# Delta-rule attention and a multiplicative FFN on one core: odd heads' keys, X and masked scores back on their own partitions, and another order of steps

## The chip, the cores and the metric

One core of one Trainium2 chip. A core has five engines that run side by side, each through its own instructions in order: TensorE (PE in the profile, its weight loads PEld), VectorE (DVE), ScalarE (ACT), GpSimd (POOL) and SyncE (SP), which here only issues DMA transfers. They share SBUF, 128 partitions wide; TensorE writes to PSUM, 128 partitions by 8 banks of 512 floats. The metric is the device time of one execution in microseconds (us), as the median of several runs. All data that is computed with is float32; the inputs arrive as float64 for the weights.

## What is computed

```python
# attention: B, H, S, D = 4, 8, 768, 48; moe_w1, moe_w2: 384x1024; w3: 1024x1024; w_out: 1024x384
k_n = k / (np.linalg.norm(k, axis=-1, keepdims=True) + 1e-06)
state = np.zeros((B, H, D, D))
for t in range(S):
    kt, vt, bt = k_n[:, :, t], v[:, :, t], beta[:, :, t, None]
    y[:, :, t] = np.einsum('bhd,bhde->bhe', q[:, :, t], state)
    v_old = np.einsum('bhde,bhd->bhe', state, kt)
    state = state + bt[:, :, :, None] * np.einsum('bhd,bhe->bhde', kt, vt - v_old)
x = y.transpose(0, 2, 1, 3).reshape(B * S, H * D)      # 3072 tokens x 384
a = x @ w1
b = x @ w2
h = a * b @ w3
out = h @ w_out
```

## The kernel before

**Tiling.** The 768 time steps are cut into 12 chunks of C = 64. A tile of a chunk has 128 partitions: batch b = NR\*z + r stands with its 64 time steps on half z of the partitions, and r (2), the head h (8) and its 48 features run along the free dimension. Tiles in feature layout (KQ, S, the FFN's xT) have an even head's 48 features from partition 0 and an odd head's from partition 64. Within a chunk the recurrence becomes products: scores K·Kᵀ and K·Qᵀ, a triangular inverse T, X = T·(V − K·S) scaled by w, the new state S + Kᵀ·X, and the outputs S·Q + (masked scores)·X.

**TensorE in corners.** These products are small (contraction 48 or 64, 48 or 64 weight columns, 48 to 128 moved columns). Each is a 64x64 tile of the array; which of the four corners it uses is given by the partitions of its operands (rows) and by the partitions that it writes (columns). A float32 product shows as two records in the profile.

**What is crossed.** In this kernel the odd heads' keys of chunk m (`ktok`, loaded by `load_crossed`, L192, four DMAs a chunk), their X and their masked scores stand on the other half of the partitions. So the product that makes X (`crossed`, called in `products`, L517) reads half z and writes half (z + h) % 2; `scores` (L360 and L366) makes an odd head's two parts by two products of 64 columns, since they go to different halves; and `outputs` (L618) can issue all products of masked scores and X in the first of its two parts, where row half and bank agree. Between the two parts PE is drained. The sums of squares and the weights w are needed in both places; `across` (L251) moves the odd heads' values to the other half by two products with an identity and two VectorE copies.

**The steps.** Every piece of work is a generator: a step runs it to its next yield. `ORDER`, a text of step names written out, sets the order of the instructions on every engine; nothing is reordered after. The names: Pn converts a piece of a weight matrix (DMA of the raw float64 words; three ScalarE operations, L671 to L673, one of which takes the sign; a shift by 3 on VectorE, L675; a sum and a product on GpSimd, L677 and L678); tn transposes a piece of w3 and fn folds w3·w_out into w34 (L713, L722); kn, qn, vn, pn are loads (pn: 16 DMAs of k and q in another layout, L226); Kn and Qn transposes on TensorE for chunks 0 and 1, dn on VectorE for the others (L320); gn squares of two chunks (L266, L268) and Nn norms; sn scores; un the DMAs that gather the 32x32 diagonal blocks of two chunks for the inverse; Vn the inverse itself, 31 steps of two VectorE operations (L434, L439) on 128 blocks at once; en the corner of the inverse (four DMAs back, L464, L473, L480, L487, L494); nn the scaling of v on GpSimd (L503); cn the chain of chunk n (three calls of `products` at L517, VectorE operations between at L550, L560, L581); yn its outputs (L618, L639, and the DMAs that complete xT); auj the FFN's two first products and their product elementwise for two chunks u and 128 columns j (L742, L751, L756); oub the last product and the store (L762, L768).

**V0 and V1.** While an inverse runs its matrix can lie in SBUF (`Vb`) or in a pair of PSUM banks, with two ScalarE copies in and two out (L428, L443). Here the inverses j < 2 lie in PSUM; the pair of banks is one of two that scores, chains and outputs take in turn.

```python
        def crossed(ps, r, h, z):
            g = NP * r + h // 2
            return ps[half((z + h) % 2), h % 2, D * g : D * g + D]
```

Of the kernel before, what the change touches and what calls it, by code (L numbers as in the profile page):

```python
# [9 lines left out]
U32 = mybir.dt.uint32  # L10
ALU = mybir.AluOpType
# [26 lines left out]
P6 k0 q0 K0 g0 k1 beta K0 K0 K0 P0 P6 K0 g0 P11 g0 Q0 g0 Q0 g0 g0 g0 P6 P6 g0 q1 Q0 Q0 Q0 P0  # L38
P0 P0 K1 K1 K1 K1 P7 K1 V0 P11 beta g0 g0 k2 beta P7 N0 P7 P7 s0 s0 s0 Q1 Q1 Q1 Q1 P11 P11
s0 s0 Q1 s1 s0 s0 s1 s1 s1 P2 P2 P10 P10 P13 u0 s1 s1 u1 t3 N0 P4 P1 P13 P2 P2 V0 t3 P10 P10  # L40
t2 P13 N0 V0 V0 P4 P4 P4 P1 P1 P3 P3 P13 s1 v0 V0 t5 V0 V0 V0 t2 t5 V0 V0 P1 P3 P3 V0 V0 f1
V0 P12 P12 P12 P12 V0 V0 n0 t4 P5 P5 P14 P14 P5 P5 t4 f2 V0 V0 V0 P14 V0 V0 k3 V0 V0 P22 f1
s0 P22 P22 V0 V0 P23 P23 P23 V0 P15 p2 P15 P15 f1 f2 f2 P14 V0 t6 t6 P22 t14 t14 P23 t15 P20
P20 t15 f7 V0 V0 P21 P21 V0 V0 V0 V0 V0 V0 V0 P15 g1 g1 n0 g1 V0 V0 t7 P21 P21 d2 d2 f3 P16
f7 P16 P16 P19 t7 f3 g1 g1 P20 P20 p2 f7 d2 d2 s2 t12 t12 f3 P19 t13 g1 g1 g1 g1 V0 e0 e0 e0
e0 P8 g1 t13 N1 P9 s2 s2 s2 P16 t8 P19 e0 e0 p3 f6 s2 P8 P8 c0 c0 f6 s2 y0 e1 e1 e1 P9 P9 V1
P17 P17 P17 p3 f6 t8 y0 P19 t11 t11 P8 t0 P18 P18 d3 d3 d3 d3 v1 s3 s3 s3 P17 s3 s3 P25 t0
P9 u2 u3 V1 t9 c0 s3 s1 f4 e1 c0 t9 N1 N1 P18 e1 n1 n1 c1 c1 P18 f4 V1 V1 V1 V1 P25 P25 P25
e1 c1 f4 P26 P26 P26 P26 c1 P24 P24 t10 t10 P31 t1 V1 V1 V1 t1 V1 V1 v2 n2 n2 f0 P24 P24 P27
y1 V1 V1 V1 f0 y1 f5 c1 P27 V1 V1 V1 V1 P31 P31 P31 V1 P30 k4 P30 P30 f5 V1 P27 y1 P27 a00  # L50
P32 f0 V1 V1 f5 k5 P30 P28 V1 V1 P32 P32 P32 V1 V1 V1 V1 V1 P29 a03 a00 a03 P28 P28 a02 a01
V1 V1 g2 V1 V1 P28 g2 g2 a02 V1 V1 P29 p4 d4 P29 P29 a01 a01 a01 c1 a00 a00 V1 a02 a02 c2 g2
g2 g2 d4 p4 d4 V1 g2 V1 e2 e2 a03 d4 g2 a05 e2 c2 P33 a03 e3 P35 p5 g2 g2 N2 P33 P33 s4 s4
s4 s4 s4 a07 a05 e2 P35 e2 e2 e3 P35 P33 P35 s4 a07 a06 c2 c2 e3 P34 v3 n3 P34 a04 n3 P34 y2
y2 c2 P34 a05 c2 c3 d5 p5 d5 d5 e3 e3 d5 a04 a06 a06 c3 k6 u4 s5 s5 s5 p6 a06 s5 s5 a05 s5
u5 V2 V2 a07 a07 e3 c3 c3 a04 a04 y3 y3 c3 N2 N2 o02 o02 o02 g3 o00 o00 k7 o01 o01 V2 V2 V2
g3 V2 V2 V2 V2 V2 V2 V2 V2 V2 V2 V2 V2 V2 V2 V2 V2 V2 V2 o00 v4 n4 n4 o03 o03 y3 a17 a13 a10
a13 V2 p6 V2 V2 V2 V2 V2 V2 V2 V2 a17 a12 a12 V2 V2 e4 a10 e4 c3 a17 a15 a15 e4 a17 a13 a13
e4 c4 d6 d6 g3 e4 e4 g3 g3 a16 a16 p7 c4 c4 a11 c4 c4 c4 a15 a15 v5 a11 a12 e5 c5 d6 d6 n5
g3 a12 y4 y4 n5 g3 g3 k8 g3 c5 e5 a14 g3 N3 V3 s6 s6 s6 s6 v6 d7 d7 p7 d7 d7 a16 a16 e5 a14  # L60
a14 e5 e5 g4 e5 N3 a14 s6 s6 s7 o03 s7 s7 s7 s7 u6 u7 V3 s7 N3 a10 a10 v7 c5 c5 a11 a11 y5
y5 y5 o01 c5 c5 V3 V3 V3 V3 o10 o10 V3 V3 V3 V3 V3 V3 p8 p8 o13 V3 V3 V3 V3 a27 o13 o13 V3
V3 V3 V3 o12 V3 V3 d8 o10 V3 a27 V3 V3 V3 o12 o12 k9 V3 V3 a24 a24 V3 V3 V3 V3 V3 V3 e6 g4
g4 g4 g4 g4 o11 o11 d8 a24 a24 d8 a27 a27 g4 g4 a23 a23 e6 a23 a23 p9 d8 g4 n6 g4 c6 e6 s8
n6 c6 v8 a26 a26 N4 s8 a26 a26 s8 s8 s8 s8 e6 e6 e6 V4 a25 a25 c6 a22 a22 n8 c6 c6 c6 y6 y6
n7 e7 e7 n7 a25 a25 e7 a20 a20 d9 d9 p9 d9 d9 s9 s9 s9 p10 s9 s9 a22 a22 N4 p10 e7 e7 u8 u9
s9 N4 c7 c7 a20 a20 a21 e7 c7 k11 c7 a21 a21 a21 V4 y7 y7 y7 o23 o23 V4 V4 V4 o23 o11 c7 V4
V4 V4 k10 g5 V4 V4 V4 V4 V4 V4 V4 V4 V4 V4 o22 o22 o22 d10 d10 a37 a35 a35 V4 v9 V4 V4 V4 V4
a37 a31 a31 V4 V4 V4 a34 a34 o20 V4 n8 d10 V4 V4 V4 V4 V4 V4 V4 e8 o20 g5 g5 a35 o21 o21 c7
c8 e9 g5 g5 g5 g5 g5 g5 n9 n9 e8 d10 e8 e8 c8 a35 g5 N5 s10 v10 s10 s10 s10 s10 u10 s10 V5  # L70
e9 a37 e8 e8 a36 c8 c8 a37 p11 a36 a36 a36 p11 o20 y8 y8 c8 c8 a34 a34 e9 e9 d11 d11 a30 d11
d11 s11 s11 s11 s11 s11 s11 e9 c9 u11 a30 a30 e9 c9 c9 a30 c9 V5 a31 a31 a32 a32 y9 y9 y9 V5
V5 V5 V5 V5 V5 a33 a33 a33 n10 a33 o21 V5 V5 V5 V5 V5 V5 a32 a32 a47 a47 a40 a40 a42 o32 a41
a42 V5 V5 n10 V5 V5 V5 o32 o33 o33 a47 o32 o33 V5 V5 V5 V5 V5 V5 V5 V5 v11 n11 V5 V5 a41 n11
V5 V5 V5 V5 V5 a47 o30 o30 o30 a42 a42 a46 a40 e10 e10 e10 a46 c9 N5 o31 e10 e10 c9 c10 a40
a44 e10 c10 c10 N5 o31 o31 a44 a44 a44 a46 e11 c10 c10 y10 a45 e11 e11 c10 a45 a45 a46 a45
a41 e11 a43 y10 a43 a43 a43 e11 e11 c11 a41 o41 o41 o41 c11 c11 o40 o40 o40 c11 y11 y11 y11
o42 o42 o43 o42 a53 a53 o43 a53 a53 a52 a52 a52 a52 a50 a50 a50 a50 a54 a54 a54 a54 a55 a55
a55 a55 a51 a56 a56 a56 a51 a51 a56 a51 a57 a57 a57 o43 a57 o50 o50 o51 o52 o50 o52 o52 o51
o51 o53 o53 o53  # L80
# [4 lines left out]
def kernel(  # L85
# [107 lines left out]
    def load_crossed(src, m, dma, tag, bufs):  # L193

        t = in_turn(work, [P, NR, H, D], tag, bufs, tag)
        for z in range(2):
            for e in range(2):
                dma(
                    out=t[half(z ^ e)].rearrange("t r (a e) d -> t e (r a) d", e=2)[:, e],
                    in_=src.rearrange("(z r) (a e) t d -> z e (r a) t d", z=2, e=2)[  # L200
                        z, e, :, C * m : C * m + C, :
                    ].rearrange("g t d -> t g d"),
                )
        return t

# [36 lines left out]
    def across(src, dst):  # L242

        n = src.shape[1]
        ps = bank([P, n, NR, NP])
        odd, even = (
            x.rearrange("p c r (a e) -> p e (c r) a", e=2) for x in (src, dst)
        )
        psv = ps[:].rearrange("p c r a -> p (c r) a")
        for z in range(2):  # L250
            pe.matmul(  # L251
                psv[half(1 - z)], lhsT=ident[half(z), half(z)], rhs=odd[half(z), 1],
                start=True, stop=True,
            )
        yield
        dve.tensor_copy(out=even[:, 0], in_=odd[:, 0])
        dve.tensor_copy(out=even[:, 1], in_=psv)
        yield

    def squares(j):  # L260
        sums[j] = ss = in_turn(small, [P, 2, 2, NR, H], "ss", 1, "ss")
        for cc in range(2):
            kt = ktoks[2 * j + cc]
            for r in range(NR):
                sq = in_turn(work, [P, H, D], "sq", 1, "sq")
                pool.tensor_tensor(out=sq[:], in0=kt[:, r], in1=kt[:, r], op=ALU.mult)  # L266
                yield
                dve.tensor_reduce(out=ss[:, 1, cc, r], in_=sq[:], axis=AX.X, op=ALU.add)  # L268
                yield
        yield from across(ss[:, 1], ss[:, 0])  # L270

    def norms(j):
        ss = sums.pop(j)[:, 0]
        seed = in_turn(small, [P, 2, NR, H], "seed", 1, "seed", U32)
        dve.tensor_scalar(
            out=seed[:], in0=ss.bitcast(U32), scalar1=-0.5, scalar2=1597463007.0,
# [3 lines left out]
        for _ in range(3):  # L280
            t = in_turn(small, [P, 2, NR, H], "nt", 2, "nt")
            dve.scalar_tensor_tensor(
                out=t[:], in0=ss, scalar=-0.5, in1=r, op0=ALU.mult, op1=ALU.mult
# [8 lines left out]
        dve.tensor_tensor(out=n[:], in0=r, in1=ss, op=ALU.mult)  # L292
        dve.tensor_scalar(out=n[:], in0=n[:], scalar1=1e-6, scalar2=None, op0=ALU.add)
        inv = in_turn(small, [P, 2, NR, H], "inv", 1, "inv")
        dve.reciprocal(out=inv[:], in_=n[:])

        w = ws[j] = in_turn(small, [P, 2, 2, NR, H], "wt", 3, "wt")
        dve.tensor_tensor(out=w[:, 0], in0=inv[:], in1=inv[:], op=ALU.mult)
        dve.tensor_tensor(
            out=w[:, 0], in0=w[:, 0], in1=beta_tok[:, 2 * j : 2 * j + 2], op=ALU.mult  # L300
        )
        ns[j] = n
        yield
        yield from across(w[:, 0], w[:, 1])

    def scale_of(x, m, crossed=0):
        j, cc = divmod(m, 2)
        return x[j][:, cc] if x is ns else x[j][:, crossed, cc]
# [17 lines left out]
    def by_tensor(m, i, src):  # L326
        KQ = KQs[m] if m in KQs else new_KQ(m)
        ps = [bank([P, NR, NP, C]) for z in range(2)]
        for r in range(NR):
            for h in range(H):  # L330
                for z in range(2):
                    x = half(z if i else (z + h) % 2)
                    pe.matmul(
                        ps[z][feat(h % 2), r, h // 2, :], lhsT=src[x, r, h, :],
                        rhs=ident[x, x], start=True, stop=True,
                    )
# [14 lines left out]
    def scores(m):  # L351
        for r in range(NR):
            KQ = KQs[m]
            ps = two_banks()
            for h in range(H):
                for z in range(2):
                    x = KQ[feat(h % 2), NR * z + r, h // 2]
                    n = 128 * (h // 2)
                    if h % 2 == 0:
                        pe.matmul(  # L360
                            ps[half(z), 0, n : n + 128], lhsT=x[:, 0, :],
                            rhs=x.rearrange("p j t -> p (j t)"), start=True, stop=True,
                        )
                    else:
                        for j in range(2):
# [520 lines left out]
```

## Time and profile before

| | |
|---|---|
| median of 3 runs (lowest, highest) | 611.42 us (610.54, 613.09) |
| the profiled execution | 610.54 us, span 608.8 us |
| mean granted TensorE clock | 0.969 |
| bytes moved by DMA | 55.67 MB, 91 GB/s in the mean |
| FFN's first products, L742 | 132.7 + 131.1 us busy on PE |
| FFN's last product, L762 | 127.3 us busy on PE |

The span is the time from the first to the last instruction in one profiled execution. A busy time counts an engine as busy as long as any of its instructions runs; the ends of matmuls are modelled, so blocks of small products are best measured from their start to the start of what follows. Below, a line of the page's second part cuts the span into 40 slices of 15.2 us and gives the busy share of each in tenths.

### The profile page before, as it was taken

The numbers are of one execution on the slowest core, as the hardware profiler recorded it, in microseconds if no ns is written. First come the engines' busy times: TensorE is split into PE (matmuls) and PEld (weight loads), VectorE is DVE, ScalarE is ACT, GpSimd is POOL, SyncE is SP. The second block draws the span as 40 slices with busy tenths as digits, with TensorE's granted clock in tenths as the row PEclk, the third lists the DMA queues.
The fourth block names the chain that finished last, engine by engine and source line by source line (L and its number), as shares of the span: only waits on it lengthen the run. The fifth ranks groups of instructions, "written<-read, shape, count | busy, mean of one in ns | idle before, by whom it ended". The sixth has DMA issues, their size and how long they took to land.

```text
span 608.8 us, 17988 instructions
## 1 busy us (share of the span) xinstructions
PE 569.2 (94%) x7804; PEld 333.2 (55%) x7804; DVE 323.8 (53%) x752; ACT 183.4 (30%) x373; POOL 145.0 (24%) x150
## 2 busy tenths in 40 slices
PE   3728998989999999999999999999999999999997
PEld 3724666644566545566555655566545564654454
DVE  2659975578745954766964539675384231101100
ACT  3677656754451012211102321123210113121100
POOL 5778866576340010200031001310000000000000
PEclk9856997999999999999999999999999999999999
DMA  9678678868764342725444354253102110000001
GB/s 200 163 192 230 189 144 172 200 143 156 135 124 86 88 81 27 124 51 111 95 88 64 48 109 99 54 84 60 48 21 86 31 33 1 27 29 13 1 13 39
DMA packets 202223, 55.67 MB, mean 91 GB/s; under 512 B 192352, under 2 KB 195424, under 8 KB 202144
## 3 DMA queue, kind: packets, MB, share of 16 engines
q1 hardware_dynamic: 197952, 53.74, 41.7%
q10 hardware_dynamic: 4192, 0.79, 1.0%
q8 instruction: 61, 1.00, 0.7%
q14 instruction: 18, 0.15, 0.1%
HBM read 42.30 MB, written 11.01 MB: 88 GB/s over the span
## 4 chain that ended last, share of the span: by engine, by line
PE 71%; DMA 8%; SPq 8%; DVE 6%; POOL 2%; issue 2%; ACT 1%; POOLq 0%; DVEq 0%; ACTq 0%
PE ps_f L742 36%; PE ps_f L762 21%; SPq L226 4%; PE ps_w L517 4%; PE ps_w L618 3%; DMA raw<-in_moe_w_dram 2%; PE ps_t L487 2%; SPq L663 2%; PE ps_w L366 2%; PE ps_t L473 1%; PE ps_w L360 1%; DVE ps_w L439 1%; DVE tb L434 1%; DMA Ub<-Ud 1%; DVE w L675 1%
## 5 line engine op out<-in xcount | busy, mean ns | idle before, releaser
L742 PE MATMUL ps_f<-xT,w2s 128*128 128x512 f32 x288 | 132.7, 600 | 0.2 <-POOL w2s L678 0.2
L742 PE MATMUL ps_f<-xT,w1s 128*128 128x512 f32 x288 | 131.1, 598 | 1.6 <-DMA xT<-xT 1.6
L762 PE MATMUL ps_f<-w,ab 128*128 128x384 f32 x384 | 127.3, 488 | 0.0
L762 PEld LDWEIGHTS ps_f<-w,ab 128*128 128x128 f32 x384 | 72.3, 190 | 50.9 <-issue 3.8
L756 DVE TENSOR_TENSOR ab<-a,ps_f 128x512 f32<-128x512 f32 x48 | 32.8, 686 | 126.0 <-PE ps_f L742 123.6
L742 PEld LDWEIGHTS ps_f<-xT,w1s 128*128 128x128 f32 x288 | 53.4, 190 | 62.9 <-issue 56.6
L742 PEld LDWEIGHTS ps_f<-xT,w2s 128*128 128x128 f32 x288 | 52.8, 190 | 59.3 <-issue 55.5
L751 ACT COPY a<-ps_f 128x512 f32<-128x512 f32 x48 | 27.5, 585 | 144.8 <-PE ps_f L742 140.5
L266 POOL TENSOR_TENSOR sq<-ktok 128x384 f32<-128x384 f32 x24 | 20.6, 858 | 156.5 <-DVE ss L268 98.9
L722 PE MATMUL ps_f<-w2s,w3T 128*128 128x384 f32 x128 | 48.9, 536 | 2.1 <-ACT w3T L716 2.1
L503 POOL TENSOR_TENSOR vtok<-vtok,n 128x384 f32<-128x384 f32 x24 | 19.6, 836 | 128.7 <-DMA vtok<-in_v_dram 128.7
L434 DVE TENSOR_TENSOR tb<-Vb,Ub 128x31 f32<-128x31 f32 (+15 forms) x124 | 43.5, 351 | 7.1 <-DMA Ub<-Ud 3.1
L639 ACT COPY xT<-ps_w 48x256 f32<-48x256 f32 x96 | 30.4, 365 | 50.1 <-PE ps_w L618 35.3
L439 DVE TENSOR_TENSOR Vb<-Vb,tb 128x31 f32<-128x31 f32 (+15 forms) x124 | 43.0, 347 | 4.3
L768 ACT COPY osb<-ps_f 128x384 f32<-128x384 f32 x24 | 11.4, 479 | 109.6 <-PE ps_f L762 81.5
L722 PEld LDWEIGHTS ps_f<-w2s,w3T 128*128 128x128 f32 x128 | 25.8, 209 | 19.9 <-issue 3.9
L360 PE MATMUL ps_w<-KQ 48*64 48x128 f32 x384 | 30.9, 306 | 3.9 <-ACT KQ L343 3.4
L360 PEld LDWEIGHTS ps_w<-KQ 48*64 48x64 f32 x384 | 25.8, 152 | 9.7 <-ACT KQ L343 4.0
L366 PE MATMUL ps_w<-KQ 48*64 48x64 f32 x768 | 30.9, 241 | 0.0
L581 DVE TENSOR_TENSOR S<-S,ps_w 48x768 f32<-48x768 f32 x20 | 19.0, 949 | 19.3 <-PE ps_w L517 14.4
L366 PEld LDWEIGHTS ps_w<-KQ 48*64 48x64 f32 x768 | 28.5, 153 | 0.1
L713 PE MATMUL ps_f<-ident,w 128*128 128x128 f32 x64 | 11.4, 320 | 14.4 <-POOL w L678 12.1
(94 smaller groups left out, 642.9 us busy)
## 6 DMA issues: line engine op xcount, KB each, us to landing
raw<-in_moe_w_dram SPq DMA_DIRECT2D x16, 512.0 KB, 4.7
vtok<-in_v_dram SPq DMA_DIRECT2D x24, 192.0 KB, 4.0
raw<-in_moe_w_dram SPq DMA_DIRECT2D x24, 192.0 KB, 3.9
out_dram<-osb SPq DMA_DIRECT2D x24, 192.0 KB, 1.9
ktok<-in_k_dram SPq DMA_DIRECT2D x44, 96.0 KB, 3.2
raw<-in_moe_w_out_dram SPq DMA_DIRECT2D x8, 384.0 KB, 4.9
Ud<-U SPq DMA_DIRECT2D x48, 64.0 KB, 2.0
Ub<-Ud SPq DMA_DIRECT2D x6, 512.0 KB, 3.5
```

What stands on the lines that cost most here:

```text
L226: sync.dma_start(out=dst[quarter(2 * e + j), :, :, tb, 0:nd].rearrange("t b a d -> t (b a) d"), in_=src.rearrange("b (a e) t d -> e (b a) ...
L360: pe.matmul(ps[half(z), 0, n : n + 128], lhsT=x[:, 0, :], rhs=x.rearrange("p j t -> p (j t)"), start=True, stop=True,)
L366: pe.matmul(ps[half(z ^ j), 1, n + C * j : n + C * j + C], lhsT=x[:, 0, :], rhs=x[:, j, :], start=True, stop=True,)
L434: dve.tensor_tensor(out=tv, in0=V[:, 0 : s + 1, s : s + 1].to_broadcast([P, s + 1, n]), in1=U[:, s, s + 1 : BS].unsqueeze(1).to_broadcast( ...
L439: dve.tensor_tensor(out=o, in0=o, in1=tv, op=ALU.subtract)
L517: pe.matmul(out(ps, r, h, z), lhsT=lhs(r, h, z), rhs=rhs(r, h, z), start=True, stop=True,)
L639: act.copy(out=xT[f, p:NP:2, b : b + NR, cc, :].rearrange("p a r t -> p r a t"), in_=pyv[f, z, b : b + NR],)
L722: pe.matmul(ps[:, 0:DM], lhsT=w3Ts[jc, kc // 4][:, kc % 4 * P : kc % 4 * P + P], rhs=wo[:, kc], start=(kc == 0), stop=(kc == KF - 1),)
L742: pe.matmul(ps[:], lhsT=w[:, m, js], rhs=x[:, m].rearrange("p b c t -> p (b c t)"), start=(m == 0), stop=(m == KM - 1),)
L751: act.copy(out=a[:], in_=ps[:])
L756: dve.tensor_tensor(out=t[:], in0=a[:], in1=ps[:], op=ALU.mult)
L762: pe.matmul(ps[:, 0:DM], lhsT=abs_[u, jc][:, b * P : (b + 1) * P], rhs=w34[:, jc, :], start=(jc == 0), stop=(jc == KF - 1),)
```

## The change

The crossing is taken out. k is loaded as q and v are (`load_tok`, two DMAs a chunk). `across` is gone, and with it the second copies of the sums and of w. X is made by `by_tokens`: half z to half z, one bank for each r. `scores` makes every head's two parts by one product of 128 columns. In `outputs` the products of masked scores and X are split by the parity of the head between the two parts. The inverse lies in PSUM for j = 0 alone; V1 runs in SBUF. The conversion of weights (a sign from ScalarE, a shift on VectorE, a product on GpSimd) is the same in both kernels. `ORDER` is another one, of 1117 steps (1145 before).

```diff
-P6 k0 q0 K0 g0 k1 beta K0 K0 K0 P0 P6 K0 g0 P11 g0 Q0 g0 Q0 g0 g0 g0 P6 P6 g0 q1 Q0 Q0 Q0 P0
...
+V0 P11 k0 g0 q0 beta P11 P11 P11 g0 g0 K0 K0 K0 P1 P1 P1 P1 K0 K0 Q0 k1 g0 g0 g0 Q0 Q0 Q0 P0
...
-    def load_crossed(src, m, dma, tag, bufs):
-
-        t = in_turn(work, [P, NR, H, D], tag, bufs, tag)
-        for z in range(2):
-            for e in range(2):
-                dma(
-                    out=t[half(z ^ e)].rearrange("t r (a e) d -> t e (r a) d", e=2)[:, e],
-                    in_=src.rearrange("(z r) (a e) t d -> z e (r a) t d", z=2, e=2)[
-                        z, e, :, C * m : C * m + C, :
-                    ].rearrange("g t d -> t g d"),
-                )
-        return t
...
-    def across(src, dst):
-
-        n = src.shape[1]
-        ps = bank([P, n, NR, NP])
-        odd, even = (
-            x.rearrange("p c r (a e) -> p e (c r) a", e=2) for x in (src, dst)
-        )
-        psv = ps[:].rearrange("p c r a -> p (c r) a")
-        for z in range(2):
-            pe.matmul(
-                psv[half(1 - z)], lhsT=ident[half(z), half(z)], rhs=odd[half(z), 1],
-                start=True, stop=True,
-            )
-        yield
-        dve.tensor_copy(out=even[:, 0], in_=odd[:, 0])
-        dve.tensor_copy(out=even[:, 1], in_=psv)
-        yield
...
-        yield from across(ss[:, 1], ss[:, 0])
...
-        yield from across(w[:, 0], w[:, 1])
...
                 for z in range(2):
                     x = KQ[feat(h % 2), NR * z + r, h // 2]
-                    n = 128 * (h // 2)
-                    if h % 2 == 0:
-                        pe.matmul(
-                            ps[half(z), 0, n : n + 128], lhsT=x[:, 0, :],
-                            rhs=x.rearrange("p j t -> p (j t)"), start=True, stop=True,
-                        )
-                    else:
-                        for j in range(2):
-                            pe.matmul(
-                                ps[half(z ^ j), 1, n + C * j : n + C * j + C],
-                                lhsT=x[:, 0, :], rhs=x[:, j, :], start=True, stop=True,
-                            )
+                    pe.matmul(
+                        ps[half(z), h % 2, 128 * (h // 2) : 128 * (h // 2) + 128],
+                        lhsT=x[:, 0, :], rhs=x.rearrange("p j t -> p (j t)"),
+                        start=True, stop=True,
+                    )
...
-        if j < 2:
+        if j == 0:
...
-        def crossed(ps, r, h, z):
-            g = NP * r + h // 2
-            return ps[half((z + h) % 2), h % 2, D * g : D * g + D]
+        def by_tokens(ps, r, h, z):
+            return ps[half(z), r, D * h : D * h + D]
...
-        for e in range(2):
+        for r in range(NR):
             dve.tensor_tensor(
-                out=X[:].rearrange("p r (a e) d -> p e (r a) d", e=2)[:, e], in0=ps[:, e],
-                in1=scale_of(ws, c, 1).rearrange("p r (a e) -> p e (r a)", e=2)[:, e]
-                .unsqueeze(2).to_broadcast([P, H, D]),
-                op=ALU.mult,
+                out=X[:, r], in0=ps[:, r],
+                in1=scale_of(ws, c)[:, r].unsqueeze(2).to_broadcast([P, H, D]), op=ALU.mult,
             )
...
-                lambda r, h, z: kt[half((z + h) % 2), r, h, :],
-                lambda r, h, z: X[half((z + h) % 2), r, h, :],
+                lambda r, h, z: kt[half(z), r, h, :], lambda r, h, z: X[half(z), r, h, :],
...
-            for r in range(NR if mode == 0 else 0):
-                for a in range(NP):
-                    for h in (a, NP + a):
-                        for z in range(2):
-                            x = half((z + h) % 2)
-                            todo.append((h, z, r, X[x, r, h, :], PT[x, r, h, :]))
+            for r in range(NR):
+                for h in range(mode, H, 2):
+                    for z in range(2):
+                        todo.append((h, z, r, X[half(z), r, h, :], PT[half(z), r, h, :]))
...
-        ktoks[m] = load_crossed(k, m, dma, "ktok", 4)
+        ktoks[m] = load_tok(k, m, dma, "ktok", 4)
```

## The prediction

> **What bounds the kernel now.** I read the page's busy times and slices first, then the same busy times cut into three stretches.
>
> ```profile
> span 608.8 us, 17988 instructions
> PE 569.2 (94%) x7804; PEld 333.2 (55%) x7804; DVE 323.8 (53%) x752; ACT 183.4 (30%) x373; POOL 145.0 (24%) x150
> 0.00:60.00 60.00, 33.45 (x502) 24.89 (x503) 35.60 (x84) 38.49 (x71) 44.05 (x51) 0.74 0.85 196
> 60.00:176.00 116.00, 107.92 (x1813) 68.07 (x1811) 81.84 (x197) 64.41 (x124) 72.30 (x64) 0.97 0.75 161
> 176.00:608.80 432.80, 427.87 (x5495) 240.29 (x5492) 206.32 (x472) 80.46 (x179) 28.65 (x37) 1.00 0.29 58
> ```
>
> Each row of the last three is a stretch, its length, then PE, PEld, DVE, ACT and POOL busy, the clock, the DMA share and GB/s. PE is idle 26.6 us of the first 60, 8.1 us up to 176, and 4.9 us in the 432.8 us after. So TensorE sets the end: the time is PE's own work plus about 40 us of gaps, most of them in the first 60 us, where PE waits for converted weights and for VectorE. The chain of waits says the same: from 177 us to the end it is almost nothing but PE. What the change adds to PE's work is added to the time; what it takes from other engines counts only in the first 176 us.
>
> Next, how fast the small products go. The timeline of PE (start, length, what) shows one chunk's blocks:
>
> ```profile
> 236.05 1.15 PE L517 MATMUL ps_w<-S,KQ 48*64 48x48 f32 x64
> 237.12 1.20 PE L487 MATMUL ps_t<-TT,T 32*32 32x32 f32 x64
> 238.25 2.84 PE L742 MATMUL ps_f<-xT,w1s 128*128 128x512 f32 x6
> 241.03 1.15 PE L517 MATMUL ps_w<-R,TT 64*64 64x48 f32 x64
> 242.11 2.84 PE L742 MATMUL ps_f<-xT,w1s 128*128 128x512 f32 x6
> 244.88 0.94 PE L517 MATMUL ps_w<-X,ktok 64*48 64x48 f32 x64
> 245.74 0.70 PE L742 MATMUL ps_f<-xT,w2s 128*128 128x512 f32 x1
> ...
> 252.06 0.63 PE L618 MATMUL ps_w<-KQ,S 48*48 48x64 f32 x32
> 252.51 1.07 PE L618 MATMUL ps_w<-PT,X 64*48 64x64 f32 x64
> 253.71 0.67 PE L618 MATMUL ps_w<-KQ,S 48*48 48x64 f32 x32
> 254.20 0.24 PE L251 MATMUL ps_f<-ss,ident 64*64 64x16 f32 x4
> 254.37 0.70 PE L742 MATMUL ps_f<-xT,w1s 128*128 128x512 f32 x1
> ```
>
> I take start to next start as what a block costs PE: S,KQ 1.07; R,TT 1.08; X,ktok 0.86; TT,T 1.13. Each is 64 records (32 products, two records each). By the code the 64-row products of S,KQ, R,TT and X,ktok go round all four 64x64 corners of the array, so 64 records are 16 rounds. TT,T uses two 32x32 tiles only, so its 64 records are 32 rounds. From 64 to 48 weight columns a block falls by 0.22 us over 16 rounds, 0.86 ns a column: a round takes about 55 ns with 64 columns and 41 with 48, and 1.08 - 16 x 0.055 = 0.20 us is fixed. Tested on TT,T: 32 rounds x 32 x 0.86 ns + 0.20 = 1.08, measured 1.13. So each tile has its own pace, and a block that uses half the tiles needs twice the rounds.
>
> **The change, part by part.**
>
> *R,TT (crossed becomes by_tokens).* Today an odd head's product lands on the other half, so all four corners work. After the change rows z go to columns z: two corners only, 32 rounds. 32 x 0.055 + 0.20 = 1.96 us against 1.08: +0.88, or +0.93 if the two-tile row's extra 0.05 is kept. Times 12 chunks: +10.6 to +11.2, I take **+10.9**. Lower bound, if 48 moved columns set the pace rather than 64 weight columns: 32 x 0.041 + 0.20 = 1.51, +0.43 x 12 = +5.2. Upper bound +11.5. All of it lies on PE; ten of twelve chunks are past 176 us, and the other two lie where PE is 93% busy.
>
> *Here a rule speaks about the same line.* R,TT already writes one bank from both row halves at once (an odd and an even half on different partitions), S,KQ never does, and they take 1.08 and 1.07 us, so sharing a bank costs nothing in these rows. The Trainium skill, "TensorEngine Tiling (Array Packing)", Gotcha 1 under "Restrictions and Gotchas", has it that different row tiles can't be in the same PSUM bank at once. By it the new R,TT, both halves in bank r, would go one record at a time: 64 x 0.055 + 0.20 = 3.7 us, and the sum below would come to about 642; the row decides against it.
>
> *Outputs.* Today the X,PT products all lie in the first of two parts (252.06 to 253.71, 24 rounds), and the second has 8 rounds; together 252.06 to 254.20 = 2.14 us. After, each part has 8 rounds of KQ,S and 8 of X,PT: the same 32 rounds and the same drain. But X,PT now takes heads in steps of two, so two neighbours share a column half and a part can begin and end half filled: at most one product (two records, 0.11 us) a part. 0 to +0.22 x 12; I take half, **+1.3** (0 to +2.6).
>
> *Scores.* The odd heads' two 64-column products become one of 128. Four corners and the same columns before and after: 0. What it removes is 384 records of issue, and the block already runs at its columns' pace; bounds -1 to +0.5.
>
> *Crossing of sums and weights (across).* Twelve blocks of four records, 0.17 us each by 254.20 to 254.37: 12 x 0.17 = **-2.0** (0 to -3: some stand next to other small blocks, some cost a wait). With them go 24 small VectorE copies (0.17 to 0.75 us each). After 176 us PE covers those; in the first 25 us VectorE's chain from squares to norms to U loses about 1 us.
>
> *Loads of k.* Four DMAs a chunk become two of the double size: SP has 22 fewer issues. A block of four took 3.55 us of its queue at 45 us, so 1.8 us a chunk, hidden behind PE later on.
>
> *V1 in SBUF rather than PSUM.* ScalarE loses four copies of 0.59 us. In exchange both inputs of V1's 62 VectorE steps now lie in SBUF. What that costs beside GpSimd stands in the timelines of DVE and POOL:
>
> ```profile
> 211.69 0.41 DVE L439 TENSOR_TENSOR Vb<-Vb,tb 128x240 f32<-128x240 f32 x1
> 212.14 0.91 DVE L434 TENSOR_TENSOR tb<-Vb,Ub 128x231 f32<-128x231 f32 x1
> ...
> 211.93 1.80 POOL L503 TENSOR_TENSOR vtok<-vtok,n 128x384 f32<-128x384 f32 x2 [29.19 <-DMA vtok<-in_v_dram]
> ```
>
> The smaller step takes 0.91 us instead of 0.40, until GpSimd's instruction is over; with V in PSUM the 128x255 step at 129.96 took 0.41 under a running conversion. So every GpSimd instruction inside V1 can hold VectorE for nearly its length. The new order puts 4 conversions (2 x 1.30 us each) and one scaling of v (0.84) between V1's first and last step, the old one 8 conversions: up to 4 x 2.6 + 0.8 = 11.2 us of holding, against four conversions fewer of other VectorE work. V1 took 35 us (110.9 to 145.7) for 21.6 us of its own instructions; 21.6 + 11.2 + 2.5 for what else stands there is again 35. The next thing late would be e2, chunk 2's corner. The new order has seven FFN products of 2.6 us between V1's last step and e2's first matmul, the old one five, so PE is covered: 0, and up to +6 if V1 slips by a further 10 us.
>
> *The new order.* Counted to the first FFN product, old against new: SP issues 20 against 10 of k, 32 against 40 of kperm and qperm, 48 against 52 of weights, else equal, so two more; GpSimd conversions 29 against 28; ScalarE 2 copies of V fewer and 2 of the fold more; VectorE 15 more V1 steps of two instructions (in the old order they follow later); PE all 16 folds' halves and chunk 1's outputs in both. No engine has materially less or more to do ahead of the point where PE fills up, so I take **0** for the 35 us of gaps up to 176 us, with -5 to +6.
>
> **Sum.** 608.8 + 10.9 + 1.3 - 2.0 = 619.0 us of span. The profiled execution's time was 610.54, 1.74 us over its span, which gives 620.7; the median of the runs is 611.42, 0.9 above that execution: **621.6 us**.
>
> **Rivals.**
> - *Gaps shrink (faster).* The place is the first 60 us, 26.6 us of idle PE; the price to beat is the 10 us above, so with the 3 us that can be told it decides from 13 us of gaps gone. For it: less on VectorE's chain to U (1 us), less on SP per k. Against: the converted weights are what PE waits for there (GpSimd 44 of 60 us), and their work is the same. At 15 us gone: 606.6.
> - *Tiles have no pace of their own.* If records only cost issue, R,TT stays at 1.08 and the sum is 608.8 - 2.0 + 1.3 + 2.6 = 610.7, no change. Against: 48 columns go faster than 64 at the same count of records, and the two-tile row.
> - *V1 late.* If GpSimd's holding comes on top of V1's 35 us, e2 stalls PE and so do c2 and c3 behind it: +6 to +11, 628 to 633.
> - *The change does nothing for PE's corners:* excluded, the slices in the code set them.
>
> **How the numbers follow.** The forecast 0.74; V1 late 0.11; tiles without pace 0.07; gaps shrink 0.08. This kernel's runs differ by 0.4%, so 0.5% (3.1 us) is about what can be told from no change. The bounds added up one way give 608.8 + 5.2 - 3 - 1 - 5 + 2.6 = 607.6, the other way 608.8 + 11.5 + 2.6 + 0.5 + 6 + 2.6 = 632; not all come together, and 80% lies within **613 to 632**. Faster than 608.4: 0.08; within: 0.07; slower than 614.5: 0.85.
>
> **What would show it.** R,TT near 2.0 us a block (1.08 means I am wrong about tiles); PE's busy time up by 8 to 12 us though its records fall by 432; the outputs' two parts even, some 1.1 us each; no L251 blocks; PE idle up to 176 us between 30 and 41 us; V1's SBUF steps drawn out to 0.9 us and more beside conversions. If PE's idle in the first 60 us falls under 15, the order, not the corners, decides.

## The result, and the profile after

| | before | after |
|---|---|---|
| median of 4 runs (lowest, highest) | 611.0 us (610.54, 613.09) | 626.41 us (625.29, 628.06) |
| span of the profiled execution | 608.8 us | 624.8 us |
| PE busy, PE idle in that span | 569.2, 39.6 us | 580.9, 43.9 us |

The ratio is 1.0248, with a 95% interval from 1.0214 to 1.0281: slower, by 15.2 us of the 611.0. The first view of the page and the busy times by stretch (columns as before: PE, PEld, DVE, ACT, POOL, then clock, DMA share, GB/s) of the changed kernel:

```profile
span 624.8 us, 17044 instructions
PE 580.9 (93%) x7372; PEld 341.4 (55%) x7372; DVE 333.2 (53%) x728; ACT 180.9 (29%) x369; POOL 145.7 (23%) x150
...
0.00:60.00 60.00, 32.62 (x436) 24.65 (x437) 34.51 (x84) 38.64 (x72) 45.10 (x52) 0.99 0.90 206
60.00:176.00 116.00, 105.16 (x1622) 65.73 (x1620) 87.19 (x180) 60.61 (x116) 68.63 (x61) 0.93 0.72 151
176.00:624.80 448.80, 443.10 (x5325) 250.97 (x5316) 211.45 (x467) 81.68 (x182) 31.97 (x38) 1.00 0.29 57
```

PE has 432 records fewer and is busy 11.6 us longer. It idles 27.4, 10.8 and 5.7 us in the three stretches (26.6, 8.1 and 4.9 before), 4.4 us more in all, most of it between 60 and 176 us. So the change costs in two ways: more work on PE, and a new wait, with a lower granted clock behind it. The work, in the timeline of PE (start, length, what), at one chunk's chain and another's outputs:

```profile
201.60 0.66 PE L569 MATMUL ps_w<-KQ,S 48*48 48x64 f32 x32
...
203.94 10.59 PE L713 MATMUL ps_f<-w,ab 128*128 128x384 f32 x32
...
249.26 2.07 PE L474 MATMUL ps_w<-R,TT 64*64 64x48 f32 x64
251.26 5.43 PE L713 MATMUL ps_f<-w,ab 128*128 128x384 f32 x16
```

From start to next start R,TT takes 2.00 us (1.08 before), the outputs, two parts of a KQ,S and a PT,X block each, 2.34 (2.14). The wait, in the same view some 110 us earlier, where the first FFN products run:

```profile
140.04 2.73 PE L693 MATMUL ps_f<-xT,w2s 128*128 128x512 f32 x4 [4.11 <-POOL w2s L629]
143.93 2.07 PE L693 MATMUL ps_f<-xT,w2s 128*128 128x512 f32 x2 [1.16 <-POOL w2s L629]
145.79 3.83 PE L693 MATMUL ps_f<-xT,w1s 128*128 128x512 f32 x6
```

In brackets is the idle time before the instruction and what ended it. PE stands still for 4.11 and 1.16 us, for the conversions of w2's first pieces. In the kernel before, the same products follow each other without a gap:

```profile
130.69 10.54 PE L742 MATMUL ps_f<-xT,w1s 128*128 128x512 f32 x24 [1.60 <-DMA xT<-xT]
141.07 7.89 PE L742 MATMUL ps_f<-xT,w2s 128*128 128x512 f32 x18
```

(w2 is waited for once there, for 0.2 us, at 177 us.) About a microsecond after the first gap the granted clock falls as well: it is 0.50 from 141.2 to 147.6 us. The twelve records of the three lines (two records are one product) take 8.3 us without the gap between them; the next twelve, at a clock of 1.00, take 5.3. Why the conversions are late stands in the timelines of ScalarE, DVE and POOL:

```profile
128.50 0.67 ACT L624 ACTIVATE raw<-raw 128x512 f32<-128x512 f32 x1
...
131.78 0.42 DVE L626 TENSOR_SCALAR w2s<-w2s 128x512 uint32<-128x512 uint32 x1
...
132.57 1.39 DVE L396 TENSOR_TENSOR Vb<-Vb,tb 128x256 f32<-128x256 f32 x1
134.00 1.40 DVE L391 TENSOR_TENSOR tb<-Vb,Ub 128x255 f32<-128x255 f32 x1
...
136.68 0.42 DVE L626 TENSOR_SCALAR w2s<-w2s 128x512 uint32<-128x512 uint32 x1
...
132.33 1.35 POOL L628 TENSOR_TENSOR w2s<-w2s,raw 128x512 uint32<-128x512 uint32 x1 [8.69 <-DMA raw<-in_moe_w_dram]
...
137.23 1.34 POOL L628 TENSOR_TENSOR w2s<-w2s,raw 128x512 uint32<-128x512 uint32 x1 [2.12 <-ACT a L702]
```

ScalarE has done its part of the second piece at 129.2, but the piece's shift (L626) starts only at 136.68: it is queued on VectorE behind V1's steps, and each of GpSimd's two instructions for a piece (132.33 and 133.76 for the first) stretches one step of V1 to 1.4 us; the steps of the same size next to them, at 132.12 and 135.43, take 0.42. Four steps from 118.3 to 123.8 are stretched in the same way. The names in the two brackets of POOL mislead: what it waited for was the shift.

### The profile page after: what moved, and what is told of

The parts are those of the page before. It is cut to its first block, busy times and chain, and to the rows that moved or that the text cites. A ratio compares the mean times of both kernels' runs of the same rounds, so it can differ in the third digit from the quotient of the medians.

```text
span 624.8 us, 17044 instructions
## 1 busy us (share of the span) xinstructions
PE 580.9 (93%) x7372; PEld 341.4 (55%) x7372; DVE 333.2 (53%) x728; ACT 180.9 (29%) x369; POOL 145.7 (23%) x150
## 4 chain that ended last, share of the span: by engine, by line
PE 68%; DVE 13%; DMA 9%; SPq 4%; issue 3%; ACT 2%; POOL 1%; ACTq 0%; DVEq 0%; POOLq 0%
PE ps_f L693 33%; PE ps_f L713 18%; PE ps_w L474 6%; DVE tb L391 5%; DVE Vb L396 4%; PE ps_w L569 3%; PE ps_w L322 3%; DMA raw<-in_moe_w_dram 3%; DMA Vd<-Vb 2%; PE ps_t L430 2%; PE ps_t L444 2%; SPq L614 2%; SPq L365 1%; DMA TT<-Vd 1%; DMA ktok<-in_k_dram 1%
## 5 line engine op out<-in xcount | busy, mean ns | idle before, releaser
L693 PE MATMUL ps_f<-xT,w2s 128*128 128x512 f32 x288 | 134.3, 606 | 5.9 <-POOL w2s L629 5.3
L693 PE MATMUL ps_f<-xT,w1s 128*128 128x512 f32 x288 | 132.8, 602 | 0.0
L391 DVE TENSOR_TENSOR tb<-Vb,Ub 128x31 f32<-128x31 f32 (+15 forms) x155 | 60.0, 387 | 9.2 <-DMA Ub<-Ud 4.4
L396 DVE TENSOR_TENSOR Vb<-Vb,tb 128x31 f32<-128x31 f32 (+15 forms) x155 | 60.7, 391 | 5.3
L460 POOL TENSOR_TENSOR vtok<-vtok,n 128x384 f32<-128x384 f32 x24 | 20.9, 890 | 139.3 <-DMA vtok<-in_v_dram 128.2
L322 PEld LDWEIGHTS ps_w<-KQ 48*64 48x64 f32 x768 | 24.3, 147 | 11.3 <-issue 7.5
L331 DVE TENSOR_TENSOR U<-ps_w,wt 128x512 f32<-128x512 f32 x24 | 16.5, 688 | 16.6 <-PE ps_w L322 16.3
L474 PEld LDWEIGHTS ps_w<-R,TT 64*64 64x64 f32 x704 | 21.5, 135 | 5.2 <-issue 3.8
L628 POOL TENSOR_TENSOR w<-w,raw 128x512 uint32<-128x512 uint32 x16 | 20.8, 1299 | 13.4 <-issue 11.4
```

The source lines that it names most:

```text
L322: pe.matmul(ps[half(z), h % 2, 128 * (h // 2) : 128 * (h // 2) + 128], lhsT=x[:, 0, :], rhs=x.rearrange("p j t -> p (j t)"), start=True, s ...
L391: dve.tensor_tensor(out=tv, in0=V[:, 0 : s + 1, s : s + 1].to_broadcast([P, s + 1, n]), in1=U[:, s, s + 1 : BS].unsqueeze(1).to_broadcast( ...
L396: dve.tensor_tensor(out=o, in0=o, in1=tv, op=ALU.subtract)
L460: pool.tensor_tensor(out=nv[:, r], in0=nv[:, r], in1=scale_of(ns, c)[:, r].unsqueeze(2).to_broadcast([P, H, D]), op=ALU.mult,)
L474: pe.matmul(out(ps, r, h, z), lhsT=lhs(r, h, z), rhs=rhs(r, h, z), start=True, stop=True,)
L628: pool.tensor_tensor(out=du, in0=du, in1=lo, op=ALU.add)
```

## The experiments

The times in the table are medians; the ratio is to runs of the kernel before that were taken beside them.

| run | median, us | ratio (95% interval) |
|---|---|---|
| a_rtt4x | 622.04 | 1.0164 (1.0136 to 1.0192) |
| a_xpt | 625.02 | 1.0222 (1.0201 to 1.0243) |
| a_v1psum | 622.63 | 1.0184 (1.0153 to 1.0215) |
| a_shift | 629.15 | 1.0290 (1.0263 to 1.0316) |
| b_rtt2 | 619.44 | 1.0110 (1.0080 to 1.0140) |
| b_v1sbuf | 621.00 | 1.0141 (1.0101 to 1.0182) |
| b_corner4 | 610.54 | 0.9933 (0.9895 to 0.9971) |
| a_bank | 624.99 | 1.0204 (1.0172 to 1.0236) |
| a_three | 619.73 | 1.0096 (1.0072 to 1.0120) |
| b_best | 605.97 | 0.9876 (0.9847 to 0.9905) |
| a_best | 611.57 | 0.9958 (0.9937 to 0.9979) |
| a_oldorder | 631.02 | 1.0303 (1.0267 to 1.0339) |

**R,TT alone, in the kernel before (b_rtt2).**

```diff
-            crossed, lambda r, h, z: TT[half(z), r, h, :], lambda r, h, z: R[half(z), r, h, :]
+            lambda ps, r, h, z: ps[half(z), h % 2, D * (NP * r + h // 2) : D * (NP * r + h // 2) + D],
+            lambda r, h, z: TT[half(z), r, h, :], lambda r, h, z: R[half(z), r, h, :]
```

> The kernel before with one edit: R,TT writes half z to half z (two corners); odd heads' X then stands on the wrong half, so outputs and states of odd heads are not the reference's. If tiles have their own pace: R,TT 1.08 -> 2.00 us, +0.92 x 12 = 11.0, less some 1.8 us for chunks 0 and 1, which stand where PE waits anyway: 620.5 us (619 to 622.5). If the changed kernel's R,TT is slow for another reason (its loads of k, its order): 611.4.

The timeline of PE in this run:

```profile
412.31 2.07 PE L517 MATMUL ps_w<-R,TT 64*64 64x48 f32 x64
414.31 2.84 PE L743 MATMUL ps_f<-xT,w2s 128*128 128x512 f32 x6
```

2.00 us, with nothing else changed. The starts of this block, chunk by chunk from the fourth, show what of it reaches the end:

| chunk | 3 | 4 | 5 | 6 | 7 | 8 | 9 | 10 | 11 | span |
|---|---|---|---|---|---|---|---|---|---|---|
| before, us | 188.93 | 241.03 | 271.88 | 328.75 | 354.84 | 406.73 | 427.76 | 492.89 | 524.27 | 608.8 |
| b_rtt2, us | 189.91 | 242.93 | 274.69 | 332.49 | 359.50 | 412.31 | 433.80 | 499.84 | 532.14 | 617.6 |
| later by | 0.98 | 1.90 | 2.81 | 3.74 | 4.66 | 5.58 | 6.04 | 6.95 | 7.87 | 8.8 |

From here on every chunk but one adds its whole 0.92 us. The first three, worth 2.8, have added 1.0 at 189 us: there PE waits for other things, and some of the longer block fits into the waits. So 11.0 us of work become 8.8 in the span, and 4.9 to 8.6 in the medians.

**The bank (a_bank).**

```diff
-            return ps[half(z), r, D * h : D * h + D]
+            return ps[half(z), (r + z) % 2, D * h : D * h + D]
```

> The changed kernel with R,TT's two row halves in different banks (half z writes bank (r + z) % 2), still two corners; the batches of half 1 are swapped within X, so outputs are not the reference's. If corners set the pace and a shared bank costs nothing: R,TT stays 2.00 us, 626.4 us (625 to 628). If the shared bank is what slows the block: 1.1 to 1.5 us, 615 to 620.

Timeline of PE:

```profile
447.47 2.07 PE L474 MATMUL ps_w<-R,TT 64*64 64x48 f32 x64
449.46 2.84 PE L693 MATMUL ps_f<-xT,w1s 128*128 128x512 f32 x6
```

Still 1.99 us. The two row halves in one bank, on different partitions, cost nothing; the two idle corners do. The ratio is 0.0044 under the changed kernel's (2.7 us), with intervals that overlap: this run's wait for w2 is 3.9 us, not 5.3. So much two kernels can differ here with these blocks at the same length.

**R,TT back on four corners (a_rtt4x).** The products of r = 1 go to the other half, and VectorE brings them back while it scales.

```diff
-            return ps[half(z), r, D * h : D * h + D]
+            return ps[half(z ^ r), r, D * h : D * h + D]
...
-            for r in range(NR):
-                for h in range(H):
+            for h in range(H):
+                for r in range(NR):
...
-        for r in range(NR):
+        for r, x, y in ((0, slice(0, P), slice(0, P)), (1, half(0), half(1)), (1, half(1), half(0))):
             dve.tensor_tensor(
-                out=X[:, r], in0=ps[:, r],
+                out=X[x, r], in0=ps[y, r],
...
```

> The changed kernel with R,TT back on four corners without crossed keys: products of r = 1 go to the other half, and VectorE reads them from there in two instructions of 64 partitions (three instructions in place of two). If each tile of the array has its own pace: the R,TT block falls from 2.00 us to 1.08-1.15, 12 x 0.9 = -10.8 us, the third VectorE instruction (about 0.5 us) is hidden by FFN products: 615.6 us (612 to 618), 1.007 of the kernel before. If the 15 us of the change come from the order and VectorE's queue instead: 626 +- 2. If the way back through VectorE is on the path: 618 to 622.

Timeline of PE:

```profile
248.50 1.15 PE L474 MATMUL ps_w<-R,TT 64*64 64x48 f32 x64
249.58 5.43 PE L714 MATMUL ps_f<-w,ab 128*128 128x384 f32 x16
```

The block is back at 1.08 us, as expected; the time fell by 5.1 us (0.0084 x 611.4), not 10.8, and the span by 6.9 (that execution took 619.61 us, less than the median). By the ratio that is 621.4 us, where the expectation put a way back through VectorE on the path; but PE waits for X nowhere in this trace. Two other things ate the rest. At 224.5 us this run is only 0.16 us ahead of the changed kernel. What chunks 0 and 1 gain does not arrive: the first products of w2 start at 139.75 us (140.04 in the changed kernel), when their conversions let them, and before that this run had a stretch at a granted clock of 0.50 (98 to 102 us). By 202.6 us it is 1.3 us ahead, and a wait of 0.9 us for ScalarE at 213 us takes most of that. And the edit gave the new order of heads to S,KQ and X,ktok too, whose busy times rose from 12.8 to 13.4 and from 10.4 to 11.3 us.

**V1 in PSUM (a_v1psum).**

```diff
-        if j == 0:
+        if j < 2:
...
-f5 V1 P20 V1 V1 V1 c1 c1 y1
+f5 V1 V1 V1 P20 V1 V1 V1 c1 y1
...
```

Chunk 1's X,ktok now follows its outputs, right ahead of the first FFN product, since only one pair of PSUM banks is left while V1 runs.

> The changed kernel with V1 in PSUM again (four ScalarE copies more; chunk 1's X,ktok moved behind its outputs). If V1's steps in SBUF, drawn out to 1.3-1.4 us beside GpSimd's conversions, make the w2 shifts behind them late: no such steps, PE idle from 60 to 176 us falls from 10.8 to about 6, 621.5 us (620 to 623.5). If the new order's weight transfers or the place of the shifts behind V1 are the cause, whatever memory V1 lies in: idle stays near 10.8, 626.4 +- 1.

Timelines of DVE, POOL and PE:

```profile
127.03 0.43 DVE L624 TENSOR_SCALAR w2s<-w2s 128x512 uint32<-128x512 uint32 x1 [0.90 <-ACT w2s L620]
...
127.82 0.43 DVE L394 TENSOR_TENSOR ps_w<-ps_w,tb 128x256 f32<-128x256 f32 x1
...
127.64 1.30 POOL L626 TENSOR_TENSOR w2s<-w2s,raw 128x512 uint32<-128x512 uint32 x1 [5.75 <-ACT raw L621]
...
132.25 5.42 PE L691 MATMUL ps_f<-xT,w1s 128*128 128x512 f32 x12
137.50 2.74 PE L691 MATMUL ps_f<-xT,w2s 128*128 128x512 f32 x6
```

The same step beside the same conversion takes 0.43 us. VectorE waits for ScalarE now, the shift is done at 127.5 in place of 132.2, V1 takes 27.7 us (113.73 to 141.43) in place of 36.8, and PE goes through its FFN products without a gap. PE's idle time between 60 and 176 us is 7.0 us, the span 4.8 us shorter, the medians' ratio 0.0064 lower (3.9 us; with both intervals, between 1 and 7). The weights' transfers, the rival, were not the cause: they stand in the same order here. PE also waits 1.9 us for X (1.4 in the changed kernel) and 1.4 for R (nothing).

**The shifts earlier (a_shift).** V1 stays in SBUF; the shifts of two pieces move ahead of some of its steps.

```diff
-V1 V1 V1 V1 V1 V1 V1 P31 V1 V1 V1 V1 V1 P30 t9 k4 P31 P31 P30 f4 f4 f6 f6 V1 V1 V1 y1 P30
+V1 V1 V1 V1 P31 P30 t9 k4 P31 P30 P31 V1 V1 V1 V1 P30 V1 V1 V1 V1 f4 f4 f6 f6 V1 V1 V1 y1
```

> The changed kernel with the shifts of the first two w2 pieces moved ahead of 8 steps of V1 on VectorE, V1 still in SBUF. If the shifts' place behind V1's steps is what PE waits for at 136-140 us: the gap of 4.11 us falls under 1, the third piece then sets the end: 623.5 us (622 to 625). If the raw words' transfers are late: the gaps stay, 626.4 +- 1.

Timeline of PE:

```profile
146.33 2.08 PE L691 MATMUL ps_f<-xT,w2s 128*128 128x512 f32 x2 [7.88 <-POOL w2s L627]
```

A miss. The first gap closed, but VectorE now waited for ScalarE ahead of the moved shift, all of V1's later steps slid back, and with them the third piece's shift, to 143.02 from 140.61. One gap of 7.88 us stands in place of two of 5.27 together. Moving two shifts only passed the delay on to the third; other places for them were not tried.

**V1 in SBUF in the kernel before (b_v1sbuf).** The reverse edit, `j < 2` to `j == 0`, and four V1 steps out of the order.

> The kernel before with V1 in SBUF (four ScalarE copies less), in its own order, which has eight conversions within V1. If GpSimd's conversions hold VectorE's steps in SBUF, and this comes on top of V1's length: V1 from 35 to 45 us or more, weights and e2 behind it late, 615 to 621 us. If it is only the new order that makes V1 in SBUF costly: 611.4 +- 1.

Timelines of DVE and PE:

```profile
137.38 1.40 DVE L437 TENSOR_TENSOR Vb<-Vb,tb 128x255 f32<-128x255 f32 x1
...
141.66 1.39 DVE L432 TENSOR_TENSOR tb<-Vb,Ub 128x247 f32<-128x247 f32 x1
...
154.87 5.49 PE L740 MATMUL ps_f<-xT,w2s 128*128 128x512 f32 x6 [3.55 <-ACT a L749]
```

Two conversions in a row stretch four steps in a row, 137.38 to 143.05, and PE waits 3.6 us for ScalarE's copy of a, 2.2 for w2 and 2.8 for X, where it waited 0.2 for w2 and not at all for the others. V1 goes from 34.8 to 44.7 us and the time up by 8.6 us (6.2 to 11.1): in its own order, where the trace has eight conversions inside V1 against five in the new one, the edit costs more, by the medians some twice as much.

**Outputs (a_xpt).**

```diff
-                for h in range(mode, H, 2):
+                for h in (mode, NP + mode, mode + 2, NP + mode + 2):
```

> The changed kernel with the heads of X,PT in each part of the outputs taken in turn from both column halves (h = mode, mode + 4, mode + 2, mode + 6). If a part's beginning and end half filled is what costs the 0.20 us a chunk: outputs 2.34 -> 2.14 us, 12 x 0.2 = -2.4: 624.0 us (623 to 625.5). If the two parts cost the same whatever the order: 626.4.

From start to next start the outputs take 2.27 us (201.64 to 203.91 us in the timeline of PE): a third of the 0.20 comes back, 12 x 0.07 = 0.8 us. The ratios say 1.6, with intervals that overlap, so the time alone shows nothing. What the other 0.13 is, is open.

**The three together (a_three).** a_v1psum, a_xpt, and a_rtt4x with the order of heads changed for R,TT alone.

> The changed kernel with three costs taken out together: R,TT on four corners through VectorE (the order of heads changed for this block alone), V1 in PSUM, X,PT's heads in turn from both column halves. If the three causes are apart and add up as measured singly: 626.4 - 5.0 - 3.9 - 0.8 = 616.7 us. If, with V1's waits gone, the R,TT blocks of the first chunks and the undisturbed loops of the other blocks count too: another 3 us off, 613.5. If the new order costs nothing by itself, as the prediction had it: the kernel before less 2.0 for the crossing and plus 1.6 for outputs, 611 us. Above 616 the order itself is worth some 5 us.

0.0096 x 611.4 = 5.9 us over the kernel before (4.4 to 7.3), that is 617.3: the single gains add up (616.7 expected by them), and no more. The execution profiled took 616.69 us, less than the median. PE's busy time is 569.7 us, that of the kernel before, so the block costs are gone; 45.3 us of idle time against 39.6 is what is left. Of it 3.9 us is chunk 1's outputs waiting for X, an effect of the moved X,ktok (1.9 in a_v1psum; here PE gets there 1.0 us earlier and X comes 1.0 later, 0.7 of it because VectorE makes it in three instructions, 1.69 us in place of 1.01).

**The old order (a_oldorder).** All of the changed code, V1 in PSUM, with `ORDER` of the kernel before.

> The changed kernel's code with V1 in PSUM, in the order of steps of the kernel before (the steps of the crossing do nothing there). If the new order costs nothing by itself, as the prediction had it: the time of the changed kernel with V1 in PSUM, 622.6 us (621 to 624). If the order is the missing part: the kernel before plus 7 for R,TT as measured there, plus 1 to 2.4 for outputs, less 2 to 3.6 for the crossing: 615.5 to 618.5, and the order is worth the rest, some 4 to 7 us.

Neither: 630 us by the ratio, 7 more than the same code in the new order. The view of PE's waits after 176 us, all of them (line, what it waited for, us in total, times, longest):

```profile
PE ps_w L475 <- issue: 3.5, 3, 1.4
PE ps_w L570 <- issue: 2.6, 2, 1.5
PE ps_t L445 <- issue: 1.6, 1, 1.6
```

Six pauses in the midst of a block, 0.8 to 1.6 us long and 7.7 us together, "for nothing that the profile shows"; the kernel before has one of 0.3 us there, the changed one at most 0.7 us. Their cause is open. They are as large as the whole difference to the new order, so what the run shows is only that the new order, for this code, is no loss; what the order is worth without them it leaves open.

**A corner on four tiles (b_corner4, b_best, a_best).** If each tile has its own pace, the corner of the inverse (T,U and TT,T, two 32x32 tiles of sixteen) should gain in either kernel. The edit, the same for both blocks:

```diff
-        for r in range(NR):
-            for h in range(H):
+        for h in range(H):
+            for r in range(NR):
                 for z in range(2):
                     pe.matmul(
-                        ps[quarter(2 * z + 1), r, h, :], lhsT=Us[m][quarter(2 * z), r, h, BS:C],
+                        ps[quarter(2 * z + 1 - r), r, h, :], lhsT=Us[m][quarter(2 * z), r, h, BS:C],
...
-            act.copy(out=X1[x], in_=ps[x])
+            for r in range(NR):
+                act.copy(out=X1[x, r], in_=ps[quarter(2 * z + 1 - r), r])
```

> The kernel before with the inverse's corner on four 32x32 tiles in place of two: products of r = 1 go to the other quarter, ScalarE's copies (four of 256 elements in place of two of 512) bring them back. If a 32x32 tile has its own pace too, as the 64x64 ones: T,U and TT,T 1.13 -> 16 x 32 x 0.86 ns + 0.20 = 0.64 us, 24 x 0.49 = -11.8, less about 2 for chunks 0 and 1: 601.5 us (600 to 605). If two tiles on the same rows share one pace: 611.4.

Timeline of PE:

```profile
234.41 0.75 PE L473 MATMUL ps_t<-T,U 32*32 32x32 f32 x64
235.10 2.84 PE L744 MATMUL ps_f<-xT,w2s 128*128 128x512 f32 x6
...
420.33 0.82 PE L360 MATMUL ps_w<-KQ 48*64 48x128 f32 x3 [2.04 <-DVE KQ L320]
...
423.29 1.40 PE L488 MATMUL ps_t<-TT,T 32*32 32x32 f32 x64
424.62 1.96 PE L519 MATMUL ps_w<-S,KQ 48*64 48x48 f32 x64
```

The block takes 0.69 us (0.64 expected), 0.44 less, 24 times. Yet the time fell by 4 us only and the runs spread from 603.34 to 612.45. In the profiled one, of 611.50 us, PE, which is early now, waits 2.04 us at 418 us for chunk 11's keys and queries, whose transfers SP issues until 417.1, and then runs slowly (the granted clock is 0.66 in the mean from 420 to 430 us, 0.50 from 424 to 428; TT,T takes 1.33 us). So b_best issues those transfers earlier:

```diff
-d10 e8 e8 c8 a35 g5 N5 s10 v10 s10 s10 s10 s10 u10 s10
+d10 p11 p11 e8 e8 c8 a35 g5 N5 s10 v10 s10 s10 s10 s10 u10 s10
...
-a37 p11 a36 a36 a36 p11 o20
+a37 a36 a36 a36 o20
```

> The kernel before with the corner on four tiles, and the loads of chunk 11's kperm and qperm moved ahead of chunk 10's scores on SP's queue. If the wait of chunk 11's scores for qperm (3 us, and half clock behind it) ate the corner's gain: 602.5 us (601 to 605), and little spread. If the gain is lost elsewhere too: 606 to 610.

> The kernel of the three repairs with the corner on four tiles as well (24 blocks by 0.44 us). If the blocks' gain comes through: 10 us under the kernel of the three repairs, 601 to 607. If PE, now faster, runs into a late load as the kernel before did: half of it, 607 to 611.

b_best is faster than both kernels: 0.9876, that is 7.6 us (5.8 to 9.4) off the kernel before, and the wait for chunk 11's keys and queries is gone from its trace. a_best, the three repairs and this corner, is 8.4 us under a_three and 2.6 under the kernel before; the block's gain comes through in part there too (8.4 of 10 us).

## Why the prediction came out as it did

The forecast was right in direction and in its main term; 621.6 is 4.8 us under the median, by one step that failed, one term that was too small, and a rest that stays open. By its steps:

- **TensorE sets the end.** Right: PE is busy 580.9 of 624.8 us.
- **R,TT, +10.9.** Right: 1.96 us said, 2.00 measured, the corners shown as the cause by b_rtt2, a_bank and a_rtt4x. Two slips: three of the twelve blocks, not two, stand ahead of 176 us (the third at 168.21), and they do not count in full: b_rtt2 shows 1.0 us for their 2.8. In the changed kernel's trace chunk 0's block even takes 3.67 us (86.46 to 90.13), at a granted clock of 0.51 behind a wait of 1.58 us; in the kernel before it is 1.19 us, at 1.00.
- **The bank rule.** Against "TensorEngine Tiling (Array Packing)", Gotcha 1, of the Trainium skill, which would have made the block 3.7 us by the prediction's estimate, the trace's row decided rightly: 2.00 us in one bank, 1.99 in two (a_bank). Two row halves on the same partitions of one bank were not tried.
- **Outputs, +1.3.** The size was off, near its upper bound: 2.34 - 2.14 = 0.20 a chunk, +2.4. Half filled ends of a part explain 0.07 of it (a_xpt).
- **Scores, 0, and the crossing, -2.0.** Where its two halves stand together, the scores block takes 1.90 us (2.03 before), and no L251 blocks are left. Neither was tried alone.
- **V1 in SBUF, 0.** This step failed. That V1 would again take about 35 us was nearly right (36.8, with five conversions inside it, not four). Wrong was "The next thing late would be e2": I looked only at what needs V1's result. What was late were the shifts of w2 that stand behind V1's steps in VectorE's queue, and through them PE's first FFN products. Putting V1 back into PSUM saved 3.9 us by the medians (a_v1psum) and 4.8 of the span. The changed kernel's trace has 5.3 us of waits for w2 and some 3 of lower clock at this place; not all of it is net cost, since a wait of 1.6 us for xT and one of 1.0 for S, in the kernel before, are gone. The rival "V1 late" had the right source, but e2 for its victim too, and a higher price (+6 to +11).
- **The new order, 0.** PE's gaps in the first 60 us stayed, as said (27.4 against 26.6). But the cost of an order by itself is not shown by these runs: in the old order the changed code is slower still (a_oldorder), by as much as its six pauses.

The spans differ by 16.0 us: 11.6 of PE's work and 4.4 of its idle time. Measured singly, R,TT is worth 8.8 us (span of b_rtt2) and V1 in SBUF 4.8 (span of a_v1psum); the outputs' blocks make 2.4, and with the 2.0 forecast for the crossing, which no run tried alone, taken off, that is 14.0. The other 2.0 us are open, and single executions differ by as much. Only a part of it was undone by runs: with three causes out, 5.9 us remain, and how much of that the repairs bring with them is open.

## What to carry to other kernels

Count how many tiles of the array a small block keeps busy: halving them nearly doubled it here (1.08 to 2.00 us), and filling idle ones was worth a longer way back through VectorE or ScalarE, which had the time. When an instruction gets longer, ask not only who needs its result but what stands behind it in its engine's queue. And a gain on the bound engine can be lost at the next load that arrives on time only for the old pace, and more of it if the clock falls behind the gap (b_corner4).

## What the runs showed of the hardware

- A VectorE step with both inputs in SBUF is held beside a GpSimd instruction of 1.3 us: 0.42 became 1.40, 0.27 became 1.42. With one of the inputs in PSUM it took 0.43.
- Tiles of the same rows and different columns run side by side at 32x32 as well: 64 records in 0.69 us on four tiles, 1.13 on two.
- VectorE and ScalarE can read PSUM on one half or quarter of the partitions and write SBUF on another: three instructions for X took 1.65 us (two, 1.01), four copies of a corner 1.49 (two, 1.16).
- The granted clock can fall 1 to 2 us after a gap: to 0.50 behind 4.11 us of idle time (141.2 to 147.6 us in the changed kernel, where six records took 3.83 us in place of 2.74), and to 0.50 behind 2.04 us in b_corner4, where the TT,T block took 1.33 us in place of 0.69. It does not always: behind 1.60 us of idle time at 130.69 us, in the kernel before, it stayed at 1.00.
- PE can pause 0.8 to 1.6 us within a block of small products (a_oldorder, six times), with nothing in the profile to say why.
